# Half block 0 of k in four contiguous pieces: another layout, another split over two queues, five narrower zero products

## The chip, the cores and the metric

The kernel runs on one core of a Trainium2 chip. The metric is the device time of one execution in microseconds; the times below are medians of several executions, and a profile is one further execution, taken by the hardware profiler. The engines are PE (matrix products; its weight loads are shown apart as PEld), DVE (vector), ACT (scalar functions), POOL and SP; SP and ACT also issue DMAs, each on a queue of its own.

## The reference

Linear attention on 4 batches of 8 heads, 576 positions and 64 elements a head, and then two feed-forward blocks on the 2304 tokens. Only the attention's first step matters here:

```python
def phi(x):
    proj = np.einsum('bhsd,md->bhsm', x, omega)
    sq = np.sum(x * x, axis=-1, keepdims=True) / 2.0
    h = proj - sq
    h = h - np.max(h, axis=-1, keepdims=True)
    return np.exp(h) / np.sqrt(m)
q_p, k_p = (phi(q_s), phi(k_s))
kv = np.einsum('bhsm,bhsd->bhmd', k_p, v)
z = np.sum(k_p, axis=2)
num = np.einsum('bhsm,bhmd->bhsd', q_p, kv)
den = np.einsum('bhsm,bhm->bhs', q_p, z)[..., None] + 1e-06
return (num / den).astype(np.float32)
```

The result, as a 2304 x 512 matrix, goes through `softplus(x @ w_in) @ w_out` and then through `((a * b) @ w3) @ w_out` with `a = x @ w1`, `b = x @ w2`.

## The kernel before

**Half blocks of k.** The keys are worked in 16 half blocks (a batch and four of its eight heads; `i` counts them, 2B = 16). Each has 512 of the 576 positions, in KT = 4 tiles of 128 (`t`); the last 64 positions of all come in a tensor of their own (krest). A half block lies in `raw[i]` (in the profile: rawk) as 128 partitions of two head pairs `p` of 512 positions. `load_k` (L300) loads it. Half blocks 1 and later come in one DMA each on SP's queue (L304). Half block 0 comes in four pieces (L307), one for each tile: pieces 0 and 2 on SP's queue, pieces 1 and 3 on ACT's, behind the load of omega (om, L695). A piece takes 128 positions of each of the two pairs, so 2 runs of 512 bytes in each partition.

**Split and projection.** `split_k` (L309) cuts half blocks 1 and later into a high part and a low part of reduced width (kt1h, kt1l and so on; three pairs of buffers, so kt1h is half block 1, 4, 7 and on). For half block 1 it does so tile by tile, the low parts on POOL; for the others at once, both parts on DVE. `k_feat` (L362) projects a tile on omega: three products of high and low parts for each pair, or, for half block 0, one product in full width. The products of one tile fill one of 8 PSUM buffers (ps). DVE takes the maximum (nmax, L349), and ACT the four exponentials of a tile (kp, L354; kpr for the last 64 positions, qp for the queries). After the last tile, `kv_sum` multiplies the kp of the half block before with v (vt), and ACT copies the sum out (kv, L389).

**Zero products.** Ahead of it all, PE multiplies a tile of zeros by itself (L699): WARM = 3 products of 128x256 whose result nobody reads. A product in full width (f32) is two instructions in the trace.

**What sets the order.** The instructions of each engine stand in an order that a scheduler makes when the kernel is built, from priorities and its own estimates; on the chip each engine works through its own in that order, and each DMA queue likewise. A change of an instruction's size therefore can move others, as shown below. Besides the keys, the stage works on the first weights of the next layer: `Job` loads them (raw<-in_w_in, L130), and ACT (L138, L139, then casts at L187 and L174) and DVE (L142, L148 and on) unpack them between the tiles. After the keys come the queries, 18 tiles of 128 tokens, which are split (qt), projected, turned (L409) and multiplied with kv; from about 150 us on the matrix stages follow.

## Time and profile before

| | us |
|---|---|
| median of 3 runs | 813.32 (813.06 to 813.55) |
| profiled execution | 814.26 |
| its span, first to last instruction | 812.1 |
| PE busy in it | 805.6 |
| DVE busy | 599.9 |
| ACT busy | 442.0 |
| DMA, mean rate over the span | 185 GB/s |

The profiled execution's own time is 2.2 us more than its span, for what lies around the program, and 0.94 us more than the median of the runs without the profiler. Busy shares are means over stages of different kinds: in the first 62 us DVE and ACT are nearly as full as PE, and later PE is the fullest by far. A time in the trace counts from the first instruction.

### The profile page before, as it was taken

What the parts mean: (1) busy time and instruction counts of PE and PEld (TensorE: products, weight loads), DVE (VectorE), ACT (ScalarE), POOL (GpSimd) and SP (SyncE); (2) the same over time, 40 slices, a digit from 0 to 9 for tenths busy, and PEclk for the clock granted to TensorE, in tenths of its full rate; (3) what the DMA queues carried; (4) which work ended last, traced back from release to release, by engine and by line L of the source; (5) the groups of instructions that cost most, each with busy time, mean ns of one, the idle gap of its engine ahead of it and who ended that gap; (6) DMA issues with size and microseconds to landing.
All of it is one profiled execution on the core that took longest, in us unless ns stands there. A gap on an engine that the chain in (4) does not pass through costs nothing.

```text
span 812.1 us, 14425 instructions
## 1 busy us (share of the span) xinstructions
PE 805.6 (99%) x5462; PEld 752.9 (93%) x5462; DVE 599.9 (74%) x1019; ACT 442.0 (54%) x862; POOL 25.8 (3%) x29
## 2 busy tenths in 40 slices
PE   9999999999999999999999999999999999999998
PEld 8989999999999998888888889999999998889998
DVE  6899899878755676755469733898988776889951
ACT  6899998557445676745456522422434223674430
POOL 3033300000000000000000000000000000000000
PEclk9999999999999999999999999999999999999999
DMA  9833535665545558687994632365565556353212
GB/s 279 339 97 107 175 98 165 208 207 216 198 148 195 184 191 264 209 262 293 320 308 149 221 117 76 147 217 182 172 217 210 188 176 235 116 171 130 78 49 79
DMA packets 75861, 150.04 MB, mean 185 GB/s; under 512 B 7184, under 2 KB 44688, under 8 KB 75792
## 3 DMA queue, kind: packets, MB, share of 16 engines
q1 hardware_dynamic: 64016, 101.55, 37.6%
q10 hardware_dynamic: 11776, 47.57, 17.3%
q8 instruction: 43, 0.70, 0.4%
q14 instruction: 26, 0.21, 0.1%
HBM read 98.24 MB, written 50.86 MB: 184 GB/s over the span
## 4 chain that ended last, share of the span: by engine, by line
PE 92%; ACT 4%; DVE 3%; DMA 1%; issue 1%; POOL 0%; DVEq 0%; ACTq 0%; POOLq 0%
PE ps L96 89%; PE ps L409 2%; ACT kp L354 2%; PE ps L439 1%; DMA xq<-xd 1%; ACT qp L354 1%; DVE s L462 0%; DVE c L517 0%; DVE nmax L349 0%; ACT f L138 0%; ACT raw L139 0%; DVE u L517 0%; DVE f L142 0%; DVE f L148 0%; ACT kv L389 0%
## 5 line engine op out<-in xcount | busy, mean ns | idle before, releaser
L96 PE MATMUL ps<-dhi,lo 128*128 128x512 f32 x256 | 99.6, 389 | 0.0
L96 PE MATMUL ps<-dlo,hi 128*128 128x512 f32 x256 | 99.6, 389 | 0.0
L96 PE MATMUL ps<-dhi,hi 128*128 128x512 f32 x256 | 99.4, 389 | 0.0
L517 DVE TENSOR_TENSOR c<-ps,u 128x384 f32<-128x384 f32 x144 | 71.5, 549 | 0.9
L642 DVE TENSOR_TENSOR dlo<-dn,dhi 128x512 fp32r<-128x512 f32 x64 | 43.8, 689 | 38.3 <-ACT dhi L641 23.7
L517 DVE TENSOR_TENSOR u<-ps,p 128x384 f32<-128x384 f32 x48 | 26.7, 556 | 56.3 <-PE ps L96 54.6
L138 ACT ACTIVATE f<-raw,bias 128x1024 f32<-128x1024 int16 (+2 forms) x43 | 46.5, 1089 | 35.6 <-DMA raw<-in_w 9.7
L641 ACT CAST dhi<-dn 128x512 fp32r<-128x512 f32 x64 | 39.3, 617 | 44.6 <-DVE dlo L642 26.6
L142 DVE SCALAR_TENSOR_TENSOR f<-raw,f 128x1024 int32<-128x1024 f32 (+2 forms) x43 | 45.1, 1049 | 23.3 <-ACT raw L139 22.7
L557 ACT ACTIVATE c<-c 128x384 f32<-128x384 f32 x72 | 35.0, 524 | 45.7 <-DVE c L517 42.2
L524 ACT COPY p<-ps 128x384 f32<-128x384 f32 x48 | 23.0, 480 | 63.3 <-PE ps L96 45.9
L96 PEld LDWEIGHTS ps<-dhi,lo 128*128 128x128 f32 x256 | 48.0, 188 | 10.1
L96 PEld LDWEIGHTS ps<-dlo,hi 128*128 128x128 f32 x256 | 48.0, 188 | 10.0
L96 PEld LDWEIGHTS ps<-dhi,hi 128*128 128x128 f32 x256 | 48.0, 188 | 9.8
L349 DVE TENSOR_REDUCE nmax<-ps 128x4 f32<-128x512 f32 x72 | 46.6, 682 | 6.1 <-PE ps L96 5.4
L139 ACT ACTIVATE raw<-raw,bias 128x1024 f32<-128x1024 int16 (+2 forms) x43 | 46.4, 1083 | 0.5
L148 DVE SCALAR_TENSOR_TENSOR f<-raw,f 128x1024 int32<-128x1024 int32 (+2 forms) x43 | 45.0, 1046 | 0.5
L354 ACT ACTIVATE qp<-ps,nmax 128x128 f32<-128x128 f32 x144 | 44.3, 542 | 1.1 <-DVE nmax L349 1.1
L354 ACT ACTIVATE kp<-ps,nmax 128x128 f32<-128x128 f32 x128 | 35.6, 485 | 7.4 <-DVE nmax L349 7.2
L96 PE MATMUL ps<-xs1h,thi 128*128 128x384 f32 x96 | 32.3, 336 | 0.2 <-DVE c L517 0.2
L96 PE MATMUL ps<-xs2h,thi 128*128 128x384 f32 x96 | 32.3, 336 | 0.0
L96 PE MATMUL ps<-xs2l,thi 128*128 128x384 f32 x96 | 32.3, 336 | 0.0
(257 smaller groups left out, 2342.3 us busy)
## 6 DMA issues: line engine op xcount, KB each, us to landing
dn<-gd SPq DMA_DIRECT2D x64, 256.0 KB, 4.2
raw<-in_w ACTq DMA_DIRECT2D x16, 1023.8 KB, 5.8
gd<-c SPq DMA_DIRECT2D x80, 192.0 KB, 3.5
pd<-c SPq DMA_DIRECT2D x48, 192.0 KB, 2.3
raw<-in_w_out ACTq DMA_DIRECT2D x10, 767.8 KB, 4.8
raw<-in_w_in ACTq DMA_DIRECT2D x6, 1023.8 KB, 5.2
rawq<-in_q SPq DMA_DIRECT2D x18, 256.0 KB, 2.9
xd<-xs SPq DMA_DIRECT2D x18, 256.0 KB, 2.9
```

The lines of the kernel that those rows point to most:

```text
L96: nc.tensor.matmul(out=o, lhsT=a, rhs=b, start=start, stop=stop, **kw)
L138: nc.scalar.activation(out=self.f, in_=top, func=AF.Relu, scale=TOP, bias=bias[:, 0:1])
L139: nc.scalar.activation(out=self.words(1, F32, 2), in_=top, func=AF.Identity, scale=TOP, bias=bias[:, 1:2])
L142: nc.vector.scalar_tensor_tensor(out=self.f.bitcast(I32), in0=self.words(1, F32, 2), scalar=-2.0 ** 31, in1=self.f, op0=ALU.max, op1=ALU.min)
L148: nc.vector.scalar_tensor_tensor(out=fi, in0=self.words(0, I32, 2), scalar=13, in1=fi, op0=ALU.logical_shift_right, op1=ALU.bitwise_or,)
L349: nc.vector.tensor_reduce(out=nmax, in_=pj, axis=AX.X, op=ALU.max, negate=True)
L354: nc.scalar.activation(out=dst[:, h, :], in_=pj[:, h, :], func=AF.Exp, bias=nmax[:, h:h + 1])
L517: nc.vector.tensor_tensor(out=z, in0=bank, in1=y, op=ALU.add)
L524: nc.scalar.copy(out=p6, in_=b1)
L557: nc.scalar.activation(out=dst, in_=src, func=AF.Softplus)
L641: nc.scalar.copy(out=hi, in_=got[m])
L642: nc.vector.tensor_tensor(out=lo, in0=got.pop(m), in1=hi.bitcast(F32), op=ALU.subtract)
```

## The change

The keys are laid out anew in memory and in SBUF: a partition of a half block holds tile after tile, and in each tile the two pairs, so that a piece of half block 0 is one run of 1 KB in each partition instead of two of 512 bytes. All that reads the keys follows: the splits (`split_k` still goes tile by tile for half block 1, now over contiguous pieces) and the projection. Of the four pieces of half block 0, only piece 1 is still issued by ACT; pieces 0, 2 and 3 are issued by SP. The zero products are five of 128x128 in place of three of 128x256.

```diff
-WARM = 3
+WARM = 5
@@ load_k
-            raw[i] = K_.tile([128, 2, 512], F32, tag="rawk", bufs=4, name="rawk")
+            raw[i] = K_.tile([128, KT, 2, 128], F32, tag="rawk", bufs=4, name="rawk")
             if i:
                 nc.sync.dma_start(out=raw[i], in_=k[i])
             else:
                 for t in range(KT):
-                    (nc.scalar if t % 2 else nc.sync).dma_start(out=raw[i][:, :, 128 * t:128 * t + 128], in_=k[i][:, :, 128 * t:128 * t + 128])
+                    (nc.scalar if t == 1 else nc.sync).dma_start(out=raw[i][:, t], in_=k[i][:, t])
@@ split_k
-            kt[i] = kt[i - KBUF] if i > KBUF else [K_.tile([128, 2, 512], FR, name=f"kt{i}{x}") for x in "hl"]
-            n = 128 if i == 1 else 512
-            for o in range(0, 512, n):
-                split(*[x[:, :, o:o + n] for x in (*kt[i], raw[i])], nc.gpsimd if i == 1 else nc.vector)
+            kt[i] = kt[i - KBUF] if i > KBUF else [K_.tile([128, KT, 2, 128], FR, name=f"kt{i}{x}") for x in "hl"]
+            n = 1 if i == 1 else KT
+            for t in range(0, KT, n):
+                split(*[x[:, t:t + n] for x in (*kt[i], raw[i])], nc.gpsimd if i == 1 else nc.vector)
@@ k_feat
-        p = project(lambda p: [x[:, p, 128 * t:128 * t + 128] for x in kt.get(i, [raw[0]])])
+        p = project(lambda p: [x[:, t, p, :] for x in kt.get(i, [raw[0]])])
@@ zero products
-        matmul(warm[:, 0:256], edge_t[:, 0:1].to_broadcast([128, 128]), edge_t[:, 0:1].to_broadcast([128, 256]), True, True)
+        matmul(warm[:, 0:128], *[edge_t[:, 0:1].to_broadcast([128, 128])] * 2, True, True)
@@ _layout
-    k_main = k[..., :512].reshape(2 * B, 2, 128, 512).transpose(0, 2, 1, 3)
+    k_main = k[..., :512].reshape(2 * B, 2, 128, KT, 128).transpose(0, 2, 3, 1, 4)
```

The scheduler's order changes with it, up to the end of the query stage; from the matrix stages on each engine's order is the same. On DVE, at half blocks 1 to 3 (kt1, kt2, kt3; nmax is the maximum of a tile; - before, + now):

```order
 L349 TENSOR_REDUCE nmax<-ps 128x4 x2
-L297 CAST kt1h<-rawk 128x2x128 x4
-L349 TENSOR_REDUCE nmax<-ps 128x4 x5
+L297 CAST kt1h<-rawk 128x256 x4
+L349 TENSOR_REDUCE nmax<-ps 128x4 x6
 L297 CAST kt2h<-rawk 128x1024
 L349 TENSOR_REDUCE nmax<-ps 128x4
 L298 TENSOR_TENSOR kt2l<-rawk,kt2h 128x1024
-L349 TENSOR_REDUCE nmax<-ps 128x4 x2
+L349 TENSOR_REDUCE nmax<-ps 128x4
 L297 CAST kt3h<-rawk 128x1024
```

One nmax that stood behind kt2l now stands ahead of kt2h. On DVE again, at half blocks 4 to 6, right behind kt1l of half block 4:

```order
+L349 TENSOR_REDUCE nmax<-ps 128x4
 L297 CAST kt2h<-rawk 128x1024
 L349 TENSOR_REDUCE nmax<-ps 128x4
 L298 TENSOR_TENSOR kt2l<-rawk,kt2h 128x1024
+L349 TENSOR_REDUCE nmax<-ps 128x4 x2
+L297 CAST kt3h<-rawk 128x1024
+L349 TENSOR_REDUCE nmax<-ps 128x4
+L298 TENSOR_TENSOR kt3l<-rawk,kt3h 128x1024
 L349 TENSOR_REDUCE nmax<-ps 128x4 x3
-L297 CAST kt3h<-rawk 128x1024
-L298 TENSOR_TENSOR kt3l<-rawk,kt3h 128x1024
-L349 TENSOR_REDUCE nmax<-ps 128x4 x4
```

Here one nmax moves ahead of kt2h, and one between kt3h and kt3l. On SP, the queue of the loads, at the first weights (raw; vt is v of a half block, rawq a tile of q):

```order
 L319 DMA vt<-in_v 128x1040
 L304 DMA rawk<-in_k 128x1024
-L130 DMA raw<-in_w_in 128x4095
-L319 DMA vt<-in_v 128x1040
-L325 DMA rawq<-in_q 128x512 x2
-L319 DMA vt<-in_v 128x1040
-L325 DMA rawq<-in_q 128x512 x2
+L319 DMA vt<-in_v 128x1040
 L130 DMA raw<-in_w_in 128x4095
 L325 DMA rawq<-in_q 128x512
```

The first weights' load moves behind a vt load, which has to wait for the products on the buffer that it fills. On ACT, where these weights are unpacked, before:

```order
12 L354 ACTIVATE kp<-ps,nmax 128x128 x10
13 L138 ACTIVATE f<-raw,bias 128x1024
14 L354 ACTIVATE kp<-ps,nmax 128x128
15 L139 ACTIVATE raw<-raw,bias 128x1024
16 L354 ACTIVATE kp<-ps,nmax 128x128 x5
17 L389 COPY kv_508<-ps 128x260
```

and now:

```order
12 L354 ACTIVATE kp<-ps,nmax 128x128 x16
13 L389 COPY kv_510<-ps 128x260
14 L138 ACTIVATE f<-raw,bias 128x1024
15 L354 ACTIVATE kpr<-ps,nmax 128x128
16 L139 ACTIVATE raw<-raw,bias 128x1024
```

L138 and L139 stand six exponentials and one copy later.

## Rows read from the trace of the kernel before

**Rows 1.** The page, part 1: busy us, share of the span, instructions.

```profile
PE 805.6 (99%) x5462; PEld 752.9 (93%) x5462; DVE 599.9 (74%) x1019; ACT 442.0 (54%) x862; POOL 25.8 (3%) x29
```

**Rows 2.** Waits of PE (total us, times, longest); timeline of its weight loads.

```profile
PE ps L409 <- ACT qp L354: 0.6, 2, 0.4
PE ps L96 <- ACT kp L354: 0.4, 1, 0.4
...
49.89 0.19 PEld L96 LDWEIGHTS ps<-vt,kp 128*64 128x64 f32 x3 [0.58 <-ACT kp L354]
...
62.29 0.14 PEld L409 LDWEIGHTS ps<-ident,qp 128*128 128x128 f32 x1 [0.59 <-ACT qp L354]
```

**Rows 3.** Timeline: start, us, engine, what, count, idle before; last row the chain.

```profile
0.92 2.93 PE L96 MATMUL ps<-edge 128*128 128x256 f32 x6 [0.92 <-POOL edge L266]
3.64 4.86 PE L96 MATMUL ps<-om,rawk 128*128 128x256 f32 x16
8.33 1.89 PE L96 MATMUL ps<-om,krest 128*128 128x256 f32 x8
...
5.57 2.52 PEld L96 LDWEIGHTS ps<-om,rawk 128*128 128x128 f32 x12 [0.74 <-DMA rawk<-in_k]
...
69.88 0.87 PE ps L409 x8
```

**Rows 4.** Issues of first loads (start, us), landings (last number), issued 0.75, 1.17, 2.75.

```profile
0.74 0.39 ACTq L695 DMA_DIRECT2D om<-in_om  x1
0.75 1.32 SPq L307 DMA_DIRECT2D rawk<-in_k  x2
...
rawk<-in_k SPq DMA_DIRECT2D x1, 128.0 KB, 2.6
...
rawk<-in_k ACTq DMA_DIRECT2D x1, 128.0 KB, 4.4
...
rawk<-in_k SPq DMA_DIRECT2D x1, 512.0 KB, 5.8
```

**Rows 5.** Stretches: busy us by engine, granted clock, DMA share, GB/s.

```profile
3.50:4.00 0.50, 0.50 (x2) 0.47 (x2) 0.00 (x0) 0.25 (x1) 0.45 (x1) 1.00 1.12 151
4.00:4.50 0.50, 0.50 (x3) 0.35 (x2) 0.00 (x0) 0.00 (x0) 0.28 (x1) 1.00 0.55 166
...
6.00:7.00 1.00, 1.00 (x6) 0.90 (x5) 0.47 (x2) 0.69 (x3) 0.00 (x0) 1.00 0.97 364
```

**Rows 6.** Timeline of DVE; the last row is PE's.

```profile
2.84 0.29 DVE L702 TENSOR_SCALAR om<-om 128x256 f32<-128x256 f32 x1 [1.94 <-DMA om<-in_om]
...
8.58 1.99 DVE L297 CAST kt1h<-rawk 128x256 fp32r<-128x256 f32 x4 [1.08 <-DMA rawk<-in_k]
...
14.08 0.68 DVE L349 TENSOR_REDUCE nmax<-ps 128x4 f32<-128x512 f32 x1
14.68 1.21 DVE L298 TENSOR_TENSOR kt2l<-rawk,kt2h 128x1024 fp32r<-128x1024 f32 x1
...
22.47 0.69 DVE L297 CAST kt1h<-rawk 128x1024 fp32r<-128x1024 f32 x1 [1.11 <-DMA rawk<-in_k]
...
16.05 0.28 PE L96 MATMUL ps<-omh,kt2l 128*128 128x256 f32 x1
```

**Rows 7.** Timeline of ACT, 24 to 34 us.

```profile
25.66 1.14 ACT L354 ACTIVATE kp<-ps,nmax 128x128 f32<-128x128 f32 x4 [1.40 <-DVE nmax L349]
27.39 3.21 ACT L354 ACTIVATE kp<-ps,nmax 128x128 f32<-128x128 f32 x12 [0.59 <-DVE nmax L349]
...
31.05 2.69 ACT L354 ACTIVATE kp<-ps,nmax 128x128 f32<-128x128 f32 x10 [0.17 <-DVE nmax L349]
33.56 1.31 ACT L138 ACTIVATE f<-raw,bias 128x1024 f32<-128x1024 int16 x1
```

**Rows 8.** DMA issues (KB, us to landing): issued at 22.78, and at 27.48.

```profile
raw<-in_w_in SPq DMA_DIRECT2D x1, 1023.8 KB, 8.4
...
vt<-in_v SPq DMA_DIRECT2D x1, 520.0 KB, 5.0
```

## The prediction

> **What bounds the kernel now.** I read the page's busy shares first: PE is busy 805.6 of 812.1 us [rows 1]. A change can therefore give only what PE waits for, or what its products take, and this change touches the first microseconds. Next come the waits of PE. Outside the launch they are few: 0.4 us for ACT's kp (the exponentials of k) and 0.6 us in two waits for qp (those of q) [rows 2]; the weight-load rows place the first at 49.89 and the last at 62.29 us [rows 2]. Third, the start. Six instructions of the zero products (three products, two instructions each) run from 0.92, and the first product of k's half block 0 follows at 3.64 [rows 3]: 2.72 us, of which 0.16 is the pipeline's filling, so 0.427 each. The eight instructions on krest, of the same 128x256, take 1.89 us with 0.38 for the last alone, 0.216 apart [rows 3]. So TensorE runs at its lower level (1.2 GHz) at first and at the upper (2.4 GHz) later. The rise falls in half block 0's second tile, whose weight load starts at 5.57 after a DMA wait [rows 3]; I put it at 5.7. The granted-clock column prints 1.00 even there [rows 5], so I go by the spacing.
>
> Half block 0 has four tiles (t = 0 to 3), four instructions each. Tile 0 needs piece 0 and the scaled omega. The piece is issued at 0.75 and takes 2.6 us, so 3.35 [rows 4]; omega is ready at 2.84 + 0.29 = 3.13 [rows 6]. Both lie under the zero products, which hold PE until 3.64 [rows 3]. Tile 0 ends at 3.64 + 4 x 0.427 = 5.34; tile 1 starts at 5.57, on the ACT queue's piece, 4.4 us after its issue [rows 3, 4]. That is 0.23 us of idle PE.
>
> Lastly DVE and ACT, since PE depends on them in the first 62 us. DVE stops 1.08 us at 8.58 for half block 1, and 1.11 us at 22.47 for half block 4 [rows 6]. ACT waits 1.40 and 0.59 us for nmax, at 25.66 and 27.39 [rows 7], and then is packed until it releases PE at 62.29.
>
> **The change, step by step.**
>
> *Zero products.* Five of 128 columns make ten instructions. Eight 128x128 f32 instructions take 0.87 us at the upper level, 0.109 each [rows 3], half of 0.216; so at the lower level 0.213. They end at 0.92 + 0.16 + 10 x 0.213 = 3.21, where the six end at 3.64.
>
> *Piece 0 and tile 0.* Each piece becomes 128 runs of 1 KB in place of 256 of 512 B. The nearest row is omega's load, also 128 runs of 1 KB: its issue takes 0.39 us, against 1.32 for two pieces [rows 4]. I take a landing near 3.0, between 2.8 and 3.35. Then omega decides: 3.13, and some 0.25 for the release, the weight load and the filling, so about 3.4 (bounds 3.3 and 3.64).
>
> *Tile 1.* Piece 1 is issued by ACT after omega and is now alone there. It is needed at about 5.1; with half the runs I expect it before 4. The wait of 0.23 goes (bounds 0 and 0.23).
>
> *Sum at the head.* From 3.40, (5.7 - 3.40) / 0.427 = 5.4 of the eight instructions of tiles 0 and 1 run at the lower level, the other 2.6 take 0.56, and tile 1 ends at 6.26. Before, krest starts at 8.33 after two tiles of 8 x 0.216, so tile 1 ended at 6.60. PE gains 0.34 us.
>
> *Half block 1, and DVE's order.* The load of half block 1 lands 5.8 us after its issue at 2.75 [rows 4]. Ahead of it DMA slumps: 151 and 166 GB/s from 3.5 to 4.5, against 364 from 6 to 7 [rows 5]. I read the slump as the price of the short runs. If it goes, (364 - 158) GB/s over 1.0 us is 0.21 MB, or 0.57 us. Bounds: 0.36 later, as SP's queue has one more piece of 131 KB ahead of it (at 364 GB/s), and 1.08 earlier, all that DVE waits there. I take 0.57, by the nearest row. DVE's order has one more reduction (nmax, 0.60 from one start to the next) ahead of kt2l, the low part of half block 2. kt2l ends at 14.68 + 1.21 = 15.89 now [rows 6], so then at 15.89 + 0.60 - 0.57 = 15.92, and PE could use it at about 15.97. PE takes it at 16.05 now [rows 6] and would come at 15.71. So PE waits 0.26, and 0.08 of the 0.34 is left.
>
> *ACT's lead.* At half block 4, DVE now does kt1h, kt1l, kt2h and only then the nmax that ACT takes at 25.66. In the changed order that nmax stands before kt2h, and another before kt3l. ACT's twelve exponentials in 3.21 us [rows 7] are 1.0 us a tile of four. Before, the fifth tile starts at 31.05 [rows 7] and the sixth ends at 33.06. With DVE's steps in the new order (the same durations, from the same 22.47) the fifth's nmax is ready 1.26 earlier, right when ACT has done the fourth and the kv copy, but the sixth's, behind kt3l, only 0.1 earlier, at 31.5; ACT takes it at once and ends at 32.54. That is 0.5 of lead, plus 0.57 if half block 4 lands as much earlier as half block 1 (DMA is packed between the two): 1.07. After this ACT is packed in both orders, with the same work until 62 us; L138 (the first w_in job) only stands 1.8 us later.
>
> *What PE gets of it.* At 49.89 PE waits 0.4; ACT is 1.07 earlier and PE 0.08, so the wait goes, and likewise the two of 0.6 together. PE's lead becomes 0.08 + 0.4 + 0.6 = 1.08, the same as ACT's 1.07. From 62 us on PE is nearly without waits, and the matrix stages have the same order of products, so the lead reaches the end.
>
> *What costs nothing.* The splits of contiguous pieces have the same elements; kt1l on POOL stays hidden behind the products on krest, whose 1.89 us [rows 3] is also what it would cost if they no longer covered it. The interleaving of half block 1's first two tiles on PE moves no work. SP's third piece costs some 0.4 us of issue, and the two old ones save as much. Waits that the changed q order may add or remove are bounded by 0.3 either way, the size of one such wait [rows 2].
>
> The sum: 1.1 us. Against the profiled execution that is 814.26 - 1.1 = 813.2 and a span of 811.0; the median of the runs shown is 0.94 below the profiled one, so **812.2**.
>
> **The rivals.**
>
> *Short runs are not what slows DMA.* For it: in the slump two queues, omega and krest were mixed, and the DMA share is near full in part of it. Against it: the rate doubles once the short pieces are through [rows 5]. With 0 in place of 0.57, kt2l is ready at 16.54, PE falls 0.5 behind, ACT leads by 0.5 from the order alone, and PE's three waits make up for it: 813.3 - 0.5 = **812.8**. Beside this stands the Trainium skill, "DMA: Bandwidth & Descriptors", section "Specifications": it gives 512 B as the least size for full line rate. By that rule 512 B runs are as good as 1 KB ones and this rival holds. The trace speaks against it, with 151 GB/s in the slump.
>
> *ACT's lead is lost before 49 us*, because DVE's reductions, not ACT, set the pace: DVE has two low-part subtractions ahead of reductions in the changed order near 50 us. Then PE's waits stay and only 0.1 is left: **813.2**.
>
> *The first weights come late.* SP now issues raw<-in_w_in after the vt load that waits for PE, so at about 27.8 rather than 22.78. It took 8.4 us when it was issued behind other loads, and the vt load of 27.48 took 5.0 [rows 8]: landing between 32.8 and 36.2. L138 stands at 33.56 now [rows 7], and would be reached at 33.56 + 1.77 - 1.07 = 34.3. Up to that landing it costs nothing; at the worst ACT stops 1.9 us with all exponentials queued behind, and PE loses 1.9 - 1.07: **814.1**. I expect 33.3.
>
> *The clock rises later* (the one that ends slower beyond doubt). The zero products end 0.4 us earlier and PE idles 0.2 before tile 0; now it idles 0.23 later instead. If the rise came only after krest, the 2.6 + 8 + 8 instructions that I count at 0.216 would cost 0.211 more each: 3.9 us, less 0.34 and the 1.0 of waits that a late PE no longer has, so 813.3 + 2.6 = **815.9**. It overtakes the gain once the rise is some 3 us late. Against it: idle time before the rise is the same to 0.05 us. The Trainium skill, "TensorE: Matmul & The Clock Gate", Part 1, says that the number of slow products varies between runs of one kernel. The three runs shown lie within 0.5 us; no run here shows more.
>
> *More than I count goes*: if another 0.7 of the 6.5 us that PE idles in all [rows 1] is freed by the new order, **811.5**.
>
> **How the numbers follow.** Forecast 0.45 (811.7 to 812.7); DMA no faster 0.19; lead lost 0.16; weights late 0.06; clock late 0.05, of which 0.03 is above 814.9; more goes 0.09. The range 811.6 to 813.6 leaves out the late weights, the late clock and most of the last. A measurement of this kernel tells about 0.2% from no change, 1.6 us: faster means below 811.7, slower above 814.9. Faster takes the last rival and the forecast's edge, 0.13; slower 0.03; the same 0.84.
>
> **What would show it.** Zero products ending at 3.2 and the first product near 3.4; no DMA wait at tile 1, krest's start at about 8.0; kt1h on DVE at about 8.0; PE's first kt2l product between 15.7 and 16.0; ACT's waits near 25 us shorter; no wait of PE for kp or qp until 62 us, where it is 1.1 earlier. I am wrong if kt1h still starts at 8.6 (first rival), if PE still waits near 49 and 62 us (second), if L138 waits for DMA (third), or if krest starts after 8.3 (fourth).

## The result: slower by 0.5%, and the profile after

The changed kernel takes 817.21 us (median of 6 executions, 816.86 to 819.32) where the kernel before takes 813.36 on the same chip: a ratio of 1.0051, 95% interval 1.0038 to 1.0064. The forecast was 812.2, and its range ended at 813.6. The profiled execution is the longest of the six: 819.32 us, span 817.1, so some 2 us of what its trace shows stand above the median.

A word is used throughout: the **lag** of PE is the start of a product in one trace less the start of the same product in the trace of before. It tells where time was lost, without regard to which engine was waited for.

The page's first part, for the changed kernel, against [rows 1]:

```profile
PE 807.5 (99%) x5466; PEld 754.3 (92%) x5466; DVE 599.1 (73%) x1019; ACT 441.8 (54%) x862; POOL 26.4 (3%) x29
```

PE is busy 1.9 us longer, although its zero products are shorter, and it idles 3.1 us longer. Its waits, against [rows 2] (total us, times, longest):

```profile
PE ps L96 <- DVE den L427: 1.5, 2, 1.0
...
PE ps L409 <- ACT qp L354: 0.8, 2, 0.4
PE ps L96 <- DVE c L517: 0.6, 1, 0.6
PE ps L96 <- DVE om L702: 0.6, 1, 0.6
PE ps L96 <- ACT kpr L354: 0.4, 1, 0.4
PE ps L96 <- DVE kt2l L298: 0.3, 1, 0.3
```

The waits for qp that were to go are still there. The waits for omega (om), for a reciprocal of the query stage (den) and for kpr and kt2l are new. Now the start, first on PE, against [rows 3], then on DVE, against [rows 6] (timeline: start, us, engine, what, count, idle before):

```profile
0.91 2.50 PE L96 MATMUL ps<-edge 128*128 128x128 f32 x10 [0.91 <-POOL edge L266]
3.97 5.38 PE L96 MATMUL ps<-om,rawk 128*128 128x256 f32 x16 [0.56 <-DVE om L702]
9.18 0.59 PE L96 MATMUL ps<-om,krest 128*128 128x256 f32 x2
```

```profile
3.62 0.29 DVE L702 TENSOR_SCALAR om<-om 128x256 f32<-128x256 f32 x1 [2.71 <-DMA om<-in_om]
...
10.46 2.00 DVE L297 CAST kt1h<-rawk 128x256 fp32r<-128x256 f32 x4 [2.11 <-DMA rawk<-in_k]
```

The ten zero instructions are issued as fast as counted (the last slot ends near 3.2, and its result is through at 3.41), but omega now reaches DVE at 3.62 in place of 2.84, so PE stands idle for 0.56 us and tile 0 starts at 3.97, later than before (3.64). The rests (the products on krest) start at 9.18 in place of 8.33. Half block 1 comes to DVE 1.9 us later. The DMA's stretches (us, busy by engine, granted clock, DMA share, GB/s), against [rows 5]:

```profile
4.00:4.50 0.50, 0.50 (x1) 0.47 (x2) 0.24 (x1) 0.00 (x0) 0.17 (x1) 1.00 0.78 174
4.50:5.00 0.50, 0.50 (x3) 0.35 (x2) 0.00 (x0) 0.00 (x0) 0.50 (x1) 1.00 0.77 201
...
9.00:9.50 0.50, 0.50 (x4) 0.45 (x3) 0.00 (x0) 0.50 (x3) 0.00 (x0) 1.00 0.93 141
```

The slump near 4 us is there without one packet of 512 bytes, and a second one stands at 9 us; before has that too. Later, on SP and ACT at the first weights (issues, the load's us to landing, and ACT's wait), against [rows 7, 8]:

```profile
29.28 0.33 SPq L319 DMA_DIRECT2D vt<-in_v  x1
29.66 0.95 SPq L130 DMA_DIRECT2D raw<-in_w_in  x1
```

```profile
raw<-in_w_in SPq DMA_DIRECT2D x1, 1023.8 KB, 8.2
```

```profile
37.88 1.25 ACT L138 ACTIVATE f<-raw,bias 128x1024 f32<-128x1024 int16 x1 [1.57 <-DMA raw<-in_w_in]
```

The load goes out at 29.66 in place of 22.78, lands at 37.85, and ACT stops 1.57 us for it. Last, the query stage, on DVE and on PE's weight loads:

```profile
71.69 0.15 DVE L426 TENSOR_SCALAR den<-ps 128x4 f32<-128x4 f32 x1
73.95 0.43 DVE L297 CAST qth<-rawq 128x512 fp32r<-128x512 f32 x1 [2.11 <-DMA rawq<-in_q]
74.30 0.17 DVE L427 RECIPROCAL den<-den 128x4 f32<-128x4 f32 x1
```

```profile
75.11 1.04 PEld L96 LDWEIGHTS ps<-kv,qpt 128*64 128x64 f32 x32 [0.76 <-PE ps L96]
...
79.38 0.19 PEld L96 LDWEIGHTS ps<-omh,qt 128*128 128x128 f32 x1 [1.13 <-PE ps L96]
```

DVE stands 2.11 us in front of the first half (qth) of a tile of q that has not landed, and the reciprocal of den, which has all it needs, is queued behind. PE waits for that reciprocal twice, 1.5 us in all by its waits above (the weight loads name the PE product they follow, the product itself names den).

The lag of PE draws it together: +0.85 at the rests, +1.89 at half block 2, +1.79 at 22 us, +2.35 at 64.6, +4.27 at 88, then between +4.0 and +4.4 up to 620 us, and +4.8 at the end. The last step is a wait of 0.6 us for DVE's c (L517, in the matrix stages) at 629 us; it comes there in several of the profiles, of either order, in differing size.

### The profile page after: what moved, and what is told of

Its sections match the earlier page's. It is cut to its first block, busy times and chain, and to the rows that moved or that the text cites. A ratio compares the mean times of both kernels' runs of the same rounds, so it can differ in the third digit from the quotient of the medians.

```text
span 817.1 us, 14427 instructions
## 1 busy us (share of the span) xinstructions
PE 807.5 (99%) x5466; PEld 754.3 (92%) x5466; DVE 599.1 (73%) x1019; ACT 441.8 (54%) x862; POOL 26.4 (3%) x29
## 4 chain that ended last, share of the span: by engine, by line
PE 88%; ACT 4%; DMA 3%; DVE 3%; issue 1%; SPq 0%; DVEq 0%; ACTq 0%
PE ps L96 86%; PE ps L409 2%; ACT kp L354 1%; PE ps L439 1%; DMA raw<-in_w_in 1%; DMA rawk<-in_k 1%; DMA w3f<-f 1%; DVE nmax L349 1%; ACT qp L354 1%; DMA rawq<-in_q 0%; ACT f L138 0%; ACT raw L139 0%; DVE f L148 0%; DVE c L517 0%; ACT kpr L354 0%
## 5 line engine op out<-in xcount | busy, mean ns | idle before, releaser
L517 DVE TENSOR_TENSOR c<-ps,u 128x384 f32<-128x384 f32 x144 | 71.6, 551 | 0.9
L138 ACT ACTIVATE f<-raw,bias 128x1024 f32<-128x1024 int16 (+2 forms) x43 | 46.2, 1081 | 40.0 <-DMA raw<-in_w 9.6
L517 DVE TENSOR_TENSOR u<-ps,p 128x384 f32<-128x384 f32 x48 | 26.7, 556 | 54.9 <-PE ps L96 53.3
L139 ACT ACTIVATE raw<-raw,bias 128x1024 f32<-128x1024 int16 (+2 forms) x43 | 46.2, 1080 | 0.5
L179 DVE TENSOR_TENSOR lo<-f,hi 128x512 fp32r<-128x512 f32 (+2 forms) x43 | 29.4, 705 | 4.2 <-ACT hi L174 4.1
```

What stands on the lines that cost most here:

```text
L138: nc.scalar.activation(out=self.f, in_=top, func=AF.Relu, scale=TOP, bias=bias[:, 0:1])
L139: nc.scalar.activation(out=self.words(1, F32, 2), in_=top, func=AF.Identity, scale=TOP, bias=bias[:, 1:2])
L179: nc.vector.tensor_tensor(out=self.lo[:, a:b], in0=self.f[:, a:b], in1=self.hi[:, a:b].bitcast(F32), op=ALU.subtract)
L517: nc.vector.tensor_tensor(out=z, in0=bank, in1=y, op=ALU.add)
```

## The experiments

Two theories stood at the start. **The data** (theory head in the first expectations, theory A in the later ones): the third piece on SP's queue (or omega's lateness) makes what follows land late, and that carries on. **The order** (theory order, later theory B): the scheduler writes another order of instructions (as shown with the change), and that order has waits of its own. What makes them separable is that the order depends on few things: the layout alone keeps the order of before, the zero products alone nearly so, and the third piece on SP brings the new one. The expectations call PE TensorE, DVE VectorE, ACT ScalarE and SP SyncE.

The summary first. "New" is the changed kernel's order or within a few rows of it on PE and ACT, "old" that of before, in the same sense. The time is the median and, beside it, the ratio to before with its interval. Next comes what PE's lag grows by from 64.6 to 88 us, how long ACT waits for the first weights, and the growth of the lag from 22 to 64.6 us.

| run | what | order | us | ratio | 64.6 to 88 | ACT | 22 to 64.6 |
|---|---|---|---|---|---|---|---|
| changed | all | new | 817.21 | 1.0051 (1.0038 to 1.0064) | +1.9 | 1.6 | +0.6 |
| e9 | all, once more | new | 819.03 | 1.0055 (1.0035 to 1.0075) | +1.5 | 0.1 | -0.9 |
| e3 | third piece on SP | new | 817.30 | 1.0035 (1.0022 to 1.0048) | +0.9 | 0.6 | -0.6 |
| e4 | e3 and zero products | new | 817.37 | 1.0037 (1.0023 to 1.0051) | +2.1 | 0 | -1.1 |
| e5 | layout, omega in halves | new | 816.79 | 1.0029 (1.0016 to 1.0042) | +2.1 | 0.8 | -0.5 |
| e7 | all, half block 1 first | new | 818.56 | 1.0050 (1.0031 to 1.0069) | +2.1 | 1.5 | +0.5 |
| e8 | all, rests of v later | new | 818.10 | 1.0041 (1.0029 to 1.0054) | +2.0 | 0 | -0.9 |
| e13 | all, krest in two | new | 817.70 | 1.0046 (1.0031 to 1.0062) | +1.9 | 0 | -0.9 |
| e14 | e13, six q buffers | new | 818.06 | 1.0041 (1.0027 to 1.0054) | +1.3 | 1.1 | +0.4 |
| e1 | layout | old | 813.58 | 0.9993 (0.9982 to 1.0004) | 0.0 | 0 | -0.9 |
| e2 | e1 and zero products | old | 814.37 | 1.0001 (0.9988 to 1.0015) | 0.0 | 0 | -1.4 |
| e6 | all, krest on ACT | old | 815.63 | 1.0012 (1.0002 to 1.0022) | +1.1 | 0 | -1.5 |
| e10 | all, nine zero products | old | 815.59 | 1.0014 (1.0000 to 1.0028) | 0.0 | 0 | -1.2 |
| e11 | e2, seven zero products | old | 815.54 | 1.0009 (0.9995 to 1.0024) | 0.0 | 0 | -1.1 |
| e12 | zero products | old | 814.60 | 1.0009 (0.9995 to 1.0023) | +1.0 | 0 | -1.3 |
| e15 | e1, six q buffers | old | 813.09 | 0.9989 (0.9976 to 1.0002) | -0.4 | 0 | -0.4 |
| e16 | all, weights earlier | third | 813.70 | 0.9995 (0.9983 to 1.0008) | -0.4 | 0 | -1.6 |
| e17 | e16, six q buffers | third | 814.79 | 1.0012 (1.0000 to 1.0024) | +0.7 | 0 | -1.7 |

On these chips executions of one kernel lie up to 4 or 5 us apart (before: 812.1 to 817.2 in one series), so a median of six to twelve executions, as here, is good to some 1 to 1.6 us, and runs of different series are compared by their ratios. The times in the expectations were set against the 813.36 of the first series; in the series below the kernel before took 813.76 to 814.58, so a time up to some 1.2 us above its range can be due to that alone.

### Each part alone

**e1**, the layout alone: the diff of the change without its queue line and its zero products.

> The new layout alone (1 KB runs), with before's zero products and two pieces on each queue; every engine's order is that of before. Theory head (the 1 KB pieces on SP's queue overtake omega, whose landing went from 2.82 to 3.60 us, so tile 0 and all behind it come late): omega lands near 3.6, the first product on k comes 0.3 us late or not at all behind the longer zero products, krest starts 0.3 to 0.9 us later than 8.33, and the time is 813.7 to 814.5. Theory order (the moved instructions cost most of the 3.85 us): 813.0 to 813.6.

Measured: 813.58 us, 0.9993. Omega is overtaken here too (3.61), the clock rises at 6.6 and the rests start 0.46 late, but at 64.6 us PE is 0.87 ahead. The layout has no cost that these runs can tell.

**e2**, the layout and the zero products:

```diff
-WARM = 3
+WARM = 5
-    matmul(warm[:, 0:256], ...to_broadcast([128, 128]), ...to_broadcast([128, 256]), True, True)
+    matmul(warm[:, 0:128], *[...to_broadcast([128, 128])] * 2, True, True)
```

> New layout and five narrow zero products, two pieces on each queue; order as before but for the first two tiles of half block 1 on PE. Theory head: like the changed kernel at the start, krest starts at 9.0 to 9.2 us, clock rise after 7 us, time 814.2 to 815. Theory order: 813.2 to 813.8.

Measured: 814.37 us, 1.0001. PE idles 0.70 us ahead of tile 0, the rests start 1.16 late, and 0.89 ahead of before is where PE stands at 64.6 all the same. The time lies in the range of the theory of the head (814.2 to 815), but the kernel before took 813.99 in this series, so the ratio shows no loss.

**e3**, the third piece on SP's queue in the old layout, and **e4**, that with the new zero products:

```diff
-    (nc.scalar if t % 2 else nc.sync).dma_start(...)
+    (nc.scalar if t == 1 else nc.sync).dma_start(...)
```

> Three pieces on SP's queue and one on ACT's, old layout (512 B runs), before's zero products; DVE, ACT and SP orders are the changed kernel's but for a few rows. Theory order: the first weights' load is issued near 28 us and ACT waits for it 1 us or more, half block 2's low part is late, the q stage has waits of 0.5 to 0.9 us that before has not; time 815.5 to 817. Theory head: omega lands at 2.8 as before, time 813.2 to 813.8.

> Three pieces on SP's queue and five narrow zero products, old layout: every engine's order is exactly the changed kernel's, only the run length of k differs. Theory order: as the changed kernel, 816 to 817.2. Theory head: 813.2 to 814.

Measured: 817.30 us (1.0035) and 817.37 us (1.0037). One word in the queue line brings most of the loss (ratios of 1.0035 and 1.0037 against 1.0051), with omega in time (2.91 and 2.81) and 512-byte runs. Half block 1 lands at 10.0 and 10.6 us in place of 8.6, and the lag grows by 0.9 and 2.1 us in the query stage. Which of the two it is, data or order, these two runs cannot say, since both came with the third piece.

**e12**, the zero products alone (the diff of e2 on the kernel before):

> The kernel before with the five narrower zero products and nothing else: 512-byte runs, two pieces on each queue, the order of before (2 rows of VectorE's differ). Omega should land at about 2.8 us as in the kernel before, so the zero products, ending at 3.2 us, leave tile 0 to wait for piece 0 alone (3.3 us): its product at 3.4 to 3.6 us, TensorE idle for 0.1 to 0.2 us, the clock's rise at 5.5 to 7 us. Both theories, order and data, expect 813 to 814.5 us here; 816 us or more would mean that the zero products, and not the queue, carry part of the loss.

Measured: 814.60 us, 1.0009. Omega lands at 2.84 and tile 0 starts at 3.44, 0.20 earlier than before, so the gain at tile 0 (counted 0.24) is there where omega is not overtaken. It does not last: tile 1 still waits 0.13 for its piece, the clock rises at 7.2, and the rests start 0.73 late.

### Data or order

**e5** keeps two pieces on each queue, but has the new order:

```diff
-    nc.scalar.dma_start(out=om, in_=om_t)
+    nc.scalar.dma_start(out=om[:, :M], in_=om_t[:, :M])
+    nc.sync.dma_start(out=om[:, M:], in_=om_t[:, M:])
```

> The kernel of e1 (1 KB runs, two pieces on each queue, the old zero products) with omega's load cut into two halves, the second on SyncE's queue. The pieces stay two and two, but the scheduler now writes nearly the changed kernel's order of instructions (4 rows of VectorE's, 5 of ScalarE's and 3 of SyncE's differ from it, against 61, 16 and 7 from the order before). Theory A, the data: the third piece on SyncE's queue makes half block 1 land at 10.4 us in place of 8, and that alone costs the 3.5 to 4 us. It expects half block 1 by 8.6 us and 813 to 814 us. Theory B, the order: the waits of TensorE at 74 to 79 us (0.55 and 0.93 us in the changed kernel) and the late first weights come with the order, wherever the pieces lie. It expects those waits again, TensorE level with the kernel before up to 60 us, 1.5 to 2.5 us behind it at 90 us, and 815 to 816.5 us. If each does its half, the time is also 815 to 816 us, and half block 1 lands early.

Measured: 816.79 us, 1.0029. Half block 1 landed at 9.29, 0.7 later than before but 1.15 earlier than in the changed kernel, and the query stage shows the wait again (timeline of DVE):

```profile
70.55 0.15 DVE L426 TENSOR_SCALAR den<-ps 128x4 f32<-128x4 f32 x1
72.96 0.43 DVE L297 CAST qth<-rawq 128x512 fp32r<-128x512 f32 x1 [2.26 <-DMA rawq<-in_q]
73.30 0.17 DVE L427 RECIPROCAL den<-den 128x4 f32<-128x4 f32 x1
```

The order has its wait in the query stage without the third piece. The whole loss of e5 can't be put down to it, for the head is late too: the rests start 2.57 us late, and 1.2 us of that are left at 64.6.

**e6** is the converse, three pieces on SP and the old order: the first rests go to ACT's queue.

```diff
-    nc.sync.dma_start(out=krest[:, r:r + 2], ...)
+    (nc.sync if r else nc.scalar).dma_start(out=krest[:, r:r + 2], ...)
```

> The changed kernel with the first load of the rests (krest) moved from SyncE's queue to ScalarE's. Three pieces stay on SyncE's queue, but the scheduler writes the order of before on VectorE (2 rows differ), and half block 1 is issued one place earlier. Theory A and theory B both expect what was lost to come back: half block 1 by 8.5 us, no wait over 0.3 us at 72 to 80 us, 813 to 814.5 us. A third theory, that three pieces on one queue cost time in themselves (they make all that SyncE issues later), expects 816 to 817.5 us as in the changed kernel. What speaks between A and B is where TensorE's lag lies: level at 20 us in both, and at 90 us.

Measured: 815.63 us, 1.0012, between the two expectations. At 64.6 us PE is level (-0.11). In the query stage it loses 1.1 all the same, 0.54 of it in one wait for den that ends at 84.1, for DVE stands 1.65 us in front of qth here too, and 1.59 in e12, both with the old order:

```profile
70.84 0.43 DVE L297 CAST qth<-rawq 128x512 fp32r<-128x512 f32 x1 [1.65 <-DMA rawq<-in_q]
```

The order alone does not make that wait; the section on the prediction takes it apart.

**e7** issues half block 1 ahead of the rests, **e8** the rests of v behind half block 2:

```diff
-    load_krest(0)
     load_k(1)
+    load_krest(0)
```

```diff
-    load_vrest(0)
     load_k(2)
+    load_vrest(0)
```

> The changed kernel, with the load of half block 1 issued ahead of the first rests instead of behind them; the order of instructions on every compute engine is the changed kernel's to the row. Half block 1 is expected at 7.5 to 8.5 us, ahead of the stretch from 8.5 us in which every 4 KB packet takes twice as long. Theory A: with the landing the whole loss goes, 813 to 814.5 us. Theory B: TensorE's lag at 20 us falls from 2.5 us to under 1, but the waits at 74 to 79 us stay, and the time is 815 to 816.5 us. Against both: 817 us, if the lag at 20 us is absorbed anyway by 60 us.

> The changed kernel with the first load of v's rests (64 partitions, 4,160 bytes each) issued behind half block 2's load instead of ahead of it (4 rows of VectorE's order and 2 of SyncE's differ from the changed kernel). It asks whether this load is what slows every packet between 8.5 and 11 us: if so, the slow stretch moves back by the 1.3 us that half block 2's load takes or more, to begin at 9.5 us or later, and half block 1's last engine is done by 9 us instead of 10.4. If the stretch stays at 8.5 to 11 us, it has another cause. On the time: theory A 813 to 815 us if half block 1 lands by 9 us; theory B 815 to 817 us, with the waits at 74 to 79 us in place.

Measured: 818.56 us (1.0050) and 818.10 us (1.0041). Half block 1 landed at 7.9 and 8.4 us in place of 10.4, and nothing came back; both times are above what either theory expected. In e7 DVE has it in hand at 8.8, but PE's clock rises only at 10.1 and the rests start at 10.8; in e8 the lag at half block 2 is 0.7 in place of 1.9, and at the end the query stage has its 2 us all the same. That half block 1 lands late falls as the explanation of the time. On the second slump e8 says what it asked (stretches of e8, as above):

```profile
9.00:9.50 0.50, 0.50 (x4) 0.44 (x3) 0.50 (x1) 0.22 (x1) 0.50 (x2) 1.00 1.14 412
9.50:10.00 0.50, 0.50 (x4) 0.43 (x3) 0.50 (x2) 0.00 (x0) 0.50 (x2) 1.00 1.19 190
```

Where the changed kernel moves 141 GB/s, e8 moves 412; its slump begins at 9.5 us, with the rests of v. These fill 64 partitions; the slump follows them.

**e9 and e10**: the changed kernel again, and the same with nine zero products, which, by the scheduler's own ways, bring back the order of before and leave the paths of all data alone.

```diff
-WARM = 5
+WARM = 9
```

> The changed kernel once more, unaltered, so that it stands beside the next two on one chip: 816.5 to 818 us, with VectorE's wait of about 2 us for a tile of q near 74 us and TensorE's two waits of 0.5 to 0.9 us behind it.

> The changed kernel with nine zero products in place of five, and nothing else. Where the data go is the changed kernel's (three pieces on SyncE's queue, 1 KB runs), but with nine the scheduler writes the order of before: no row of VectorE's order and one each of ScalarE's and SyncE's differ from it, against 43, 14 and 9 for the changed kernel. The eighteen zero instructions at 0.213 us end near 4.9 us, 0.9 us after the tile's product could have started (3.97 us), but TensorE is then never idle, and the clock should rise by 6.5 us. Theory A (the third piece on SyncE's queue costs by the data): half block 1 again at about 10.4 us and 817 us or, with the later start, more. Theory B (the order costs): half block 1 may still come at 10.4 us and TensorE lag by 1 to 2 us at 20 us, but VectorE's wait near 74 us and TensorE's two waits are gone, and the time is 814 to 815.5 us.

Measured on one chip: 819.03 us (1.0055) and 815.59 us (1.0014). e10's time is just above the range of theory B. e10's half block 1 landed at 10.43, as late as the changed kernel's, and PE lagged 1.9 us at half block 2; e9's landed at 7.55, although it is the changed kernel itself. In the query stage (DVE, e9 first, then e10):

```profile
71.31 0.43 DVE L297 CAST qth<-rawq 128x512 fp32r<-128x512 f32 x1 [1.72 <-DMA rawq<-in_q]
```

```profile
70.27 0.70 DVE L297 CAST qth<-rawq 128x512 fp32r<-128x512 f32 x1 [0.33 <-DMA rawq<-in_q]
```

At 64.6 us e10 stands 0.51 us behind e9, at 104 us it is 1.06 ahead. With the data on the same paths the medians are 3.4 us apart; the traces of the two place 1.6 of it in the query stage, and where the rest lies they do not show. The pair is not quite clean: the four more zero products also fill PE's idle time ahead of tile 0, and the rests start 2.1 us earlier in e10. e11 below has that filling against e2, in one order, and its median is no lower (1.0009 against 1.0001), which speaks for the order as the cause here.

### Which wait of the order

**e13** (control) and **e14** give q's tiles a sixth buffer, in room that the rests of k free:

```diff
-    krest = K_.tile([128, B, 2, 128], F32, name="krest")
+    krest[r // 2] = K_.tile([128, 2, 2, 128], F32, tag="krest", bufs=1, name="krest")
@@ (its use, and the place of the second fill, change with it)
@@ e14 alone
-    raw[t] = Q_.tile([128, 512], F32, tag="rawq", bufs=5, name="rawq")
+    raw[t] = Q_.tile([128, 512], F32, tag="rawq", bufs=6, name="rawq")
```

> The control for the next kernel: the changed kernel with the rests of k in one buffer of half the size, filled twice, which frees 2 KB in each partition; the second fill is issued after the products on the first. The order is the changed kernel's (2 rows of VectorE's and 2 of SyncE's differ). Both theories expect the changed kernel's time, 816.5 to 819 us, with VectorE's wait of about 2 us for the tile of q between 70 and 74 us.

> The kernel of e13 with six buffers for the tiles of q in place of five, in the 2 KB that it freed. TensorE's order stays the changed kernel's to the row, ScalarE's to 2 rows; VectorE's changes in the query stage (47 rows). The early tile's load no longer waits for the buffer of the seventh tile (that is freed at 70.0 us in the changed kernel) but for that of the sixth (freed at 67.4, so it lands about 2.6 us earlier). If this load is what the order costs, VectorE's wait of 2 us goes or falls under 0.5, TensorE's two waits at 72 to 80 us fall under 0.3 in all, and the time is 814 to 815.5 us. If the order costs elsewhere too, the wait goes but the time stays at 816.5 us or more.

Measured: 817.70 us (1.0046) and 818.06 us (1.0041). The waits of e14, first of DVE at 64 to 92 us, then of ACT at 22 to 50 us:

```profile
DVE qth L297 <- DMA rawq<-in_q: 0.9, 2, 0.8
```

```profile
ACT f L138 <- DMA raw<-in_w_in: 1.1, 1, 1.1
```

DVE's wait falls from 2.1 to 0.9 and the query stage's share from 1.9 to 1.3. But in this run ACT also waited for the first weights, and the lag grew by 0.4 from 22 to 64.6 us where it shrank by 0.9 in e13. So the median did not move, and this experiment alone shows only that the one wait is not all. It is no clean test of that wait either: the buffer came free earlier, but qth moved forward too, so the time between the two casts stayed at 3.7 us, and the wait fell because the load took 2.6 us in place of 3.9 (more on this below).

**e15**, the sixth buffer and the new layout, in the old order:

> The kernel of e1 (1 KB runs, two pieces on each queue, the old zero products) with the two edits of e14. TensorE's order is that of before to the row, VectorE's differs in 19 rows. It had no wait over 0.35 us of TensorE between 5 and 110 us before these edits, so there is little to gain: 812.5 to 814 us; slower than that, above 815, if VectorE's new order makes waits of its own.

Measured: 813.09 us, 0.9989 (0.9976 to 1.0002): the lowest of all, and not told from before; no version among these is shown to be faster than it.

**e16** queues the work on the first weights one half block earlier; **e17** adds e14's edits:

```diff
-        if i == B:
+        if i == B - 1:
             queue += job_ops(win[:1])
```

> The changed kernel with the work on the first weights queued one half block of k earlier, so that their load is issued ahead of the last load of k and two places before the vt load that it stood behind (issue near 22 us in place of 28.7 to 30); five buffers for q's tiles, as in the changed kernel. The order around it moves too (34 rows of VectorE's, 19 of ScalarE's against the changed kernel). If the late weights are part of what the order costs, ScalarE no longer waits for them (0.6 to 1.6 us in five of the nine kernels with that order) and TensorE's lag at 64 us is 0.5 to 1 us smaller at the same head; VectorE's wait for the early tile of q near 70 to 74 us is expected to stay, with 1.5 to 2 us of TensorE's lag: 815.5 to 817 us. If the late weights cost nothing, 817 to 818.5 us.

> Both at once: the work on the first weights one half block earlier (e16) and six buffers for the tiles of q (e14). If the two waits together are what the order costs, the time is 813.5 to 815 us, with no wait of ScalarE for the weights, VectorE's wait for q's tile under 0.9 us, and TensorE's waits from 24 to 90 us under 1 us in all. If it stays at 816.5 us or more, the order costs in a place that I have not named.

Measured: 813.70 us (0.9995) and 814.79 us (1.0012). With the layout, the zero products and three pieces on SP all in place, the loss is gone. In e16, an issue of SP, then ACT, then DVE:

```profile
22.52 0.42 SPq L130 DMA_DIRECT2D raw<-in_w_in  x1
```

```profile
31.50 1.27 ACT L138 ACTIVATE f<-raw,bias 128x1024 f32<-128x1024 int16 x1
```

```profile
68.24 0.69 DVE L297 CAST qth<-rawq 128x512 fp32r<-128x512 f32 x1 [0.34 <-DMA rawq<-in_q]
```

The weights go out at 22.5 again, ACT does not wait, and DVE's wait for the tile of q is 0.34 in place of 2.1, without the sixth buffer. I had expected that wait to stay. In the new order the seventh tile's cast stands behind the weights' work and comes at 68.16 (64.65 before); POOL frees its buffer at 69.98 (66.48), and only then can the load go out that qth waits for. With the weights' work earlier the cast is at 63.34. But e16 moves 34 rows of DVE's order and 19 of ACT's, so that the weights' place is the root of both waits is the likeliest reading, not proved; that most of the loss lies in the order, and not in where the data go, is shown by e7, e8, e10 and e16 together.

### The clock and omega

**e11** fills the idle time ahead of tile 0 with seven narrow zero products (WARM = 7 in e2's kernel):

> The kernel of e2 (1 KB runs, two pieces on each queue, narrow zero products) with seven zero products in place of five: the fourteen instructions end near 4.05 us, so that they fill the 0.70 us in which TensorE stood idle for omega in e2. The order is that of before on every engine but TensorE's own zero products. The theory on the clock, that the idle time ahead of tile 0 is what put its rise off (5.7 us with no idle time, 7.4 with 0.56, 7.8 to 9.9 with 0.70), expects the rise at 5.7 to 6.8 us, TensorE's lag at the start of the rests at most 0.6 us (1.16 in e2), and 812.5 to 813.8 us, at or a little under the kernel before. If the rise comes at 7.5 us or later all the same, the idle time is not what sets it, and the time is that of e2, 814 to 814.5 us.

Measured: 815.54 us, 1.0009; its profiled execution was 812.71 and is the shortest of twelve. The time is above the expected range, but the clock rose even earlier than expected (4.9). The same shows in e10 beside the changed kernel again (e9); timeline of PE at the start:

```profile
0.92 3.95 PE L96 MATMUL ps<-edge 128*128 128x128 f32 x18 [0.92 <-POOL edge L266]
4.71 3.64 PE L96 MATMUL ps<-om,rawk 128*128 128x256 f32 x16
```

```profile
0.92 2.50 PE L96 MATMUL ps<-edge 128*128 128x128 f32 x10 [0.92 <-POOL edge L266]
4.01 6.39 PE L96 MATMUL ps<-om,rawk 128*128 128x256 f32 x16 [0.59 <-DVE om L702]
```

The same sixteen instructions take 3.64 us behind zero products that reach up to them, and 6.39 behind 0.59 us of idle time. By the trace's records of the granted clock the rise to 2.4 GHz comes at 3.8 to 7.2 us in the eight profiles in which PE stood idle for 0 to 0.31 us ahead of tile 0 (before 5.7, e1 6.6, e3 7.1, e4 6.2, e10 4.5, e11 4.9, e12 7.2, e15 3.8), and at 6.8 to 10.3 us in the eleven in which it stood 0.51 to 1.11 us (changed 7.4, e9 9.5). The two ranges overlap, and in e10 and e11 PE had more zero products as well as less idle time, so that idle time alone puts the rise off is likely, not shown. In time it is not to be told: the median of e11 is not below e2's.

## Why the prediction was wrong

**Zero products, piece 0, tile 0: the duration right, the landing wrong.** Their last slot ends near 3.2 as counted. Omega was taken over from [rows 6] as a constant, 2.84, though the change alters what runs beside it: its load is issued at the same time as piece 0's, on the other queue. With 1 KB runs SP's pieces go ahead of it: piece 0 lands at 3.40 (counted 3.0) and omega at 3.60. In all profiles with the new layout and omega whole on ACT's queue it lands at 3.6 to 4.3, with the old layout at 2.8 to 2.9. The head's 0.34 gain became a loss of 0.33 at tile 0.

**The clock.** The fourth rival had the right place and too low a chance. The rests start +0.85 late here, +2.57 at most (e5), where it priced a rise behind krest at 3.6 (3.9 less 0.34). As to the chance, its evidence against, that the idle time before the rise stays the same, hung on omega's landing. To the end its price was too high as well, since a lag at the rests is mostly regained by 64.6 us (e6: +2.20, then -0.11).

**Half block 1.** The step read the slump at 3.5 to 4.5 us as the price of 512-byte runs and priced it at 0.57 us. A slump stands there with 1 KB runs too (174 and 201 GB/s), so the first rival was right. Where half block 1 does come earlier, in e1 by 0.66 us, it is by its issue (2.12 in place of 2.75); the load takes 5.8 us in both. The Trainium skill's "DMA: Bandwidth & Descriptors", section "Specifications", has 512 bytes as the least size for the full rate; the trace agrees with it here. The landing at 10.44 lies outside my bounds (0.36 later at most): the trace marks the end of each of the 16 DMA engines' shares, and 15 are through by 8.09; the last falls into the second slump. With three pieces on SP and the other early loads in place and order this came in five of the profiles with 10.0 us or more (changed, e3, e4, e10, e13), not in e9, e14, e16 and e17; with two pieces on it in none of seven. To the end it costs little: e10 has it and the time of the old order.

**ACT's lead.** The gain of 1.0 us was to come from three waits of PE, 0.44 at 49.89, 0.28 at 58.19 and 0.36 at 62.29 (the middle one is not among [rows 2]). These were partly a thing of that one execution: e1 has the order of before to the row and shows, between 24 and 66 us, a single wait of 0.3. The profiled execution was 0.94 us above the median, and the waits that I counted on are of that size, so the sum took 0.94 off for the execution and then most of the same waits once more; this is the likely reading. It fits that the lag falls by 0.9 to 1.5 us between 22 and 64.6 us in every trace with the old order and five buffers.

**The first weights late.** The third rival had the mechanism in full: issued behind the vt load (29.66; I had 27.8, as PE was not 1.9 us late in my sum), a load of 8.2 us, ACT waiting 1.57 us. It comes and goes with the execution: ACT waits 0.6 to 1.6 us in five of the nine profiles with the new order. Where the wait is 1.1 or more the lag grows by 0.4 to 0.6 us from 22 to 64.6 us, where it is 0.1 or none it falls by 0.9 to 1.1: 1.4 us between them, where I had 1.9 at the worst. I gave it 0.06.

**The query stage: the step that failed.** "Waits that the changed q order may add or remove are bounded by 0.3 either way, the size of one such wait." The bound was the size of a wait that existed; a new wait has no such bound. In the nine profiles with the new order the lag grows by 0.9 to 2.1 us in this stage, 1.9 in the changed kernel's own.

The wait is made of a buffer that comes free too late. DVE casts the seventh tile of q (qt), POOL makes its low part behind that and so frees its buffer, SP issues the load of a later tile into it, and DVE needs that tile at qth. From the cast to the issue it is 1.8 to 2.4 us in all profiles. The rows, for before and then for the changed kernel (DVE; POOL; the tile's load, KB and us from issue to landing; last the DMA queue of the instructions from 70 to 74 us, packets, MB, share):

```profile
64.65 0.43 DVE L297 CAST qt<-rawq 128x512 fp32r<-128x512 f32 x1
67.61 0.69 DVE L349 TENSOR_REDUCE nmax<-ps 128x4 f32<-128x512 f32 x1 [0.76 <-ACT qpt L411]
69.22 1.10 DVE L297 CAST qth<-rawq 128x512 fp32r<-128x512 f32 x1
...
65.21 1.27 POOL L298 TENSOR_TENSOR qt<-rawq,qt 128x512 fp32r<-128x512 f32 x1 [0.60 <-DVE qt L297]
...
rawq<-in_q SPq DMA_DIRECT2D x1, 256.0 KB, 2.5
```

```profile
68.16 0.41 DVE L297 CAST qt<-rawq 128x512 fp32r<-128x512 f32 x1
...
68.70 1.28 POOL L298 TENSOR_TENSOR qt<-rawq,qt 128x512 fp32r<-128x512 f32 x1 [1.35 <-PE ps L409]
...
rawq<-in_q SPq DMA_DIRECT2D x1, 256.0 KB, 3.9
...
q8 instruction: 1, 0.02, 2.1%
```

Two things changed. *The room between the casts*: DVE comes to qth 4.6 us behind the first cast in before (64.65 to 69.22) and 3.7 us behind it in the changed kernel (68.16 to 71.84). The rows between them are the same, so reading the order showed nothing; but in before DVE stands idle for 0.76 us among them, and in the changed kernel, where it comes late from the weights' work, it does not. This goes with the order without exception: 3.7 us in all eight profiles with the new order and five buffers, 4.6 or 4.7 in before and in all six with the old order and five buffers. *The load*: 2.5 us in before, 3.9 in the changed kernel, 2.5 to 4.3 over all 19 profiles, and long ones come in either order (4.2 and 4.3 in e6 and e12). The wait is 1.8 + 3.9 - 3.7, or 2.0 of the 2.1 us. With the load of before it would be 0.7. So of the 2.1 us some 0.7 go with the room, and 1.4 with the load.

Why the load was long the traces show in part. In every profile 15 of its 16 shares are through within 2.7 us of the issue; what differs is the last one. In the nine profiles where a 16 KB packet of the instruction queue (q8) begins 0.9 to 1.5 us after the issue, the last share takes 3.5 to 4.3 us; in the other ten, where such a packet begins 2.3 us after it or later, 2.5 to 3.1. That is seven of the eight profiles with the new order and five buffers, and two with the old. No run moved that packet alone, so that it holds up the share is likely, not shown. The trace of before could have given about 0.5 (1.8 + 2.5 less the 3.8 that the rows between take there without the idle time), already over my bound; the length of this load in another execution it could not give.

**The sum.** In the profiled execution: 1.8 us at 22 us, 0.6 more by 64.6 (where the traces without late weights regain 0.9 or more), 1.9 in the query stage and 0.6 at 629 us make the 4.8 us of lag at the end; the span is 5.0 longer. The forecast missed by 5.0 us: 1.1 of gain that was not there, and 3.9 of loss. As to the loss, the nine runs with the new order have ratios of 1.0029 to 1.0055, the seven with the old 0.9989 to 1.0014. Compared at the same split of the pieces, the order is worth 2.3 us (e5, with its late head, against the mean of the five old ones with two pieces on SP) to 2.6 us (the other eight against e6 and e10), and the third piece on SP 1.0 to 1.3 us, each by medians that are good to 1 to 1.6 us. The traces say the like: on the mean the new order is behind the old by 1.0 us at 22 us, by 0.7 more at 64.6 and by 1.5 more at 88. The first of these is the head, where theory A has its share; how much of it reaches the end is not settled.

## What to carry to other kernels

Where a scheduler writes the order, moving one small load to another queue is an edit to the whole stage: check by a variant that keeps the order (another count of filler products did it here) before putting a loss or a gain down to the data. For each buffer that is filled again, compare the time from the instruction that frees it to the one that needs its next content with the time that the freeing, the issue and the load take, and take the load's longest time of several profiles (2.5 to 4.3 us for the same 256 KB here), not that of one; that margin, not the waits seen, bounds what a changed order can cost. And a wait seen in one profile whose time is above the median may be that execution's own: do not sell it as a gain.

## What the runs showed of the hardware

**Beside a 64-partition load the others are slow.** While the first rests of v (64 partitions, 4,160 bytes each) are under way, packets of 4 KB take 0.30 to 0.45 us in place of 0.16 and the core moves 141 to 266 GB/s in place of 350 to 412; in e8, where the load is later, the slump is later. The second such load, whose shares land from 15.6 to 18.1 us in before, has its slump too (203 GB/s from 15 to 16 us). The Trainium skill's "SBUF — State Buffer", section "Door 1: The DMA port swizzle", says that partitions 0 to 63 are reached by only 8 of 16 ports; the rate of about half agrees with it, and that the loads to all partitions suffer alongside is what the trace adds.

**Idle time ahead of the first real products goes with a later rise of the clock**, 6.8 to 10.3 against 3.8 to 7.2 us, as listed above. The same kernel varies by 2 us too (changed 7.4, e9 9.5).

**Which of two loads issued together on two queues lands first turned with the runs of one**: omega, 128 runs of 1 KB on ACT's queue, lands at 2.8 to 2.9 us beside pieces of 256 runs of 512 bytes and at 3.6 to 4.3 beside pieces of 128 runs of 1 KB, its own issue unchanged. Why was not tried.

**One share of 16 can hold up a load.** Half block 1 has 15 shares through by 8.09 us and the last at 10.44, and the tile of q above 15 within 2.6 us and the last at 3.9. With the tile of q a 16 KB instruction packet began early in the load each of the nine times that the load was long; half block 1 has no such packet beside it, and its last share falls into the slump of the rests of v.
